# Converting 64-bit weights with two VectorE passes per piece instead of three

## The chip, the cores and the metric

The kernel runs on one core of a Trainium2 chip. The metric is the device time in microseconds; with one core it is that core's time from launch to end. A core has five engines with instruction queues of their own[...]: TensorE (PE; its weight loads are listed as PEld), VectorE (DVE), ScalarE (ACT), GpSimd (POOL) and SyncE (SP), which here only issues DMAs. They meet through semaphores.

## What is computed

A thresholded attention feeds a feed-forward block with an ELU in the middle. All tensors are 32-bit floats but the two weight matrices: they come from a product of an array with a 64-bit scalar and so arrive with 64 bits per element.

```python
scores = scale * np.matmul(q, k.transpose(0, 1, 3, 2))      # 8 x 8 heads, 576 x 576, head_dim 64
thresh = np.max(scores, axis=-1, keepdims=True) - tau
scores = np.where(scores >= thresh, scores, -1000000000.0)
scores = scores - np.max(scores, axis=-1, keepdims=True)
attn = np.exp(scores)
attn = attn / (np.sum(attn, axis=-1, keepdims=True) + 1e-09)
x = np.matmul(attn, v)                                      # as (4608, 512) tokens
h = x @ w_in                                                # w_in 512 x 2048, 64 bits
g = np.where(h > 0.0, h, np.exp(np.minimum(h, 0.0)) - 1.0)
out = g @ w_out                                             # w_out 2048 x 512, 64 bits
```

## The kernel before

Work on attention is cut into steps. A step is one block of 128 queries of a pair of heads (both heads), or the last 64 queries of both heads together; a pair takes five steps (the function calls carry `pr` for the pair and `i` for the block), four pairs make one sequence, and there are eight sequences. In a step, TensorE makes the scores of the two heads (L272), VectorE their maxima (L312), ScalarE the exponentials (L321, L323), VectorE the mask, which multiplies the exponentials by the comparison with the threshold and adds up the row sums (L332), then two short instructions for the reciprocals (L338, L339), and GpSimd the normalization (L308). In the next step TensorE transposes the weights of attention (L342), ScalarE copies them out of PSUM (L358), and for every second or third step TensorE multiplies them with the values (L477, L482), which ScalarE copies out (L599, L605).

[...]In the stages that concern us, the scores of the two heads take two banks each, and these come free when VectorE's mask has read them: so the scores of a step can't start before the masks of an earlier one.

The order of all engines is written out by hand, stage by stage, under `tc.manual_schedule()`; nothing is reordered afterwards. There are these stages:

- the first sequence (20 steps, to about 101 us). TensorE has idle-looking gaps that are filled with transposes of a constant tile, at places the code gives.
- the second stage, 15 steps (about 101 to 220 us), in which the feed-forward units of the first tokens are put between the attention work: `ffn1` (L640, with the exponential L647, GpSimd's minus one at L650 and VectorE's ELU at L654) and `ffn2_plain` (L680). `SHARES` says how many halves of a unit stand at which place in a step.
- later stages, in which the weights are in place as 32-bit numbers and the feed-forward products run in a form with fewer multiplications (L1133, L1273), with a planner that gives due times.

The conversion of the weights lies in the first two stages. They come in 32 pieces of 128 x 512 elements (16 of `w_in`, 16 of `w_out`), each with its two 32-bit words per element side by side: `staged[i]` is 128 x 512 x 2, so that the low words and the high words are each read with a stride of two words. `load_w` brings them in on SP's queue, into one of four buffers (`wst`). The work on piece `i` is cut into small functions, which the hand-written order calls at different places:

- `convert_rest` (L156): ScalarE turns the low word into the 3 bits and the rounding that it adds to a 32-bit number: low word times 2^-29, as an integer, in place.
- `convert_top`, which is `convert_shift` (L167) and `convert_sign` (L172): VectorE shifts the high word left by 3 and clears the top two bits, into `wtop` (two buffers); then it sets the top two bits from the high word.
- `convert_add` (L178): GpSimd adds the low word's share, as integers.
- `convert_abs` (L183): ScalarE takes the magnitude of the high word, read as a 32-bit float, in place.
- `convert_end` (L190): VectorE multiplies the sum by the comparison of that magnitude with a small bound, which makes numbers too small to matter exactly zero, and writes the result into `w_in_sb` or `w_out_sb`. It frees the buffer for the next load.

In the first stage the order places two pieces per pair of heads: for one, `convert_top`, `convert_add`, `convert_abs` stand in the pair's last step between the maxima and the mask, with `convert_end` in the next step; for the other, `convert_shift` stands at the end of one step, `convert_sign` and `convert_add` in the next, before its first mask. In this way 6 pieces are done. In the second stage each of the first 13 steps takes two pieces, `now[0]` and `now[1]`. The core of that step's order:

```python
if not behind_max: convert_top(now[0])          # else behind the maxima
finish_units(carried, slice(0, 2))              # exp, minus one of the step before
if not behind_max: convert_add(now[0])
early_ = ffn_halves(share[0])
...                                             # max_of, exp_of, bound_of for both heads; then the ELU
convert_abs(now[0])
after = ffn_halves(share[1])
convert_top(now[1]); convert_add(now[1]); convert_abs(now[1])
parts[1]()()                                    # transposes of the step before
second = ffn_halves(share[2])
carried = ffn_halves(share[3])
for h in hs: mask_of(pr, i, h)
reciprocal_of(pr, i, hs)
normalize(*step, hs)
for x in now: convert_end(x)
finish_units(after + second, slice(2, None))    # ELUs
```

`behind_max` holds in the first step of the stage and in the steps that also multiply with the values; there both pieces' `convert_top` stand behind the maxima, one straight after the other.

Of the kernel before, what the change touches and what calls it, by code (L numbers as in the profile page):

```python
# [10 lines left out]
FP32 = mybir.dt.float32  # L11
U32 = mybir.dt.uint32
I32 = mybir.dt.int32
AF = mybir.ActivationFunctionType
ALU = mybir.AluOpType
# [34 lines left out]
def kernel(  # L50
# [10 lines left out]
    nc = tc.nc  # L61
# [71 lines left out]
    pieces = [(moe_w_in, w_in_sb[:, j, n : n + WN], j, n) for n in range(0, DF, WN) for j in range(KJ)]  # L133
    pieces += [(moe_w_out, w_out_sb[:, f, n : n + WN], f, n) for f in range(NFT) for n in range(0, DM, WN)]
    staged, tops = {}, {}
# [16 lines left out]
    def convert_rest(i):  # L152

        if i in staged:
            lo = staged[i][:, :, 0]
            nc.scalar.mul(lo.bitcast(I32), lo, 2.0**-29)  # L156

    def convert_top(i):
        convert_shift(i)
        convert_sign(i)  # L160


    def convert_shift(i):
        if i in staged:
            hi = staged[i][:, :, 1]
            top = tops[i] = wstage.tile([P, WN], U32, name="wtop", bufs=2)
            nc.vector.tensor_scalar(top, hi, 3, 0x3FFFFFFF, ALU.logical_shift_left, ALU.bitwise_and)  # L167

    def convert_sign(i):
        if i in staged:  # L170
            hi, top = staged[i][:, :, 1], tops[i]
            nc.vector.scalar_tensor_tensor(top, hi, 0xC0000000, top, ALU.bitwise_and, ALU.bitwise_or)  # L172

    def convert_add(i):

# [3 lines left out]

    def convert_abs(i):  # L180
        if i in staged:
            mag = staged[i][:, :, 1].bitcast(FP32)
            nc.scalar.activation(mag, mag, AF.Abs)  # L183

    def convert_end(i):

        progress[1] = i + 1
        if i in staged:
            mag, top = staged.pop(i)[:, :, 1].bitcast(FP32), tops.pop(i).bitcast(FP32)
            nc.vector.scalar_tensor_tensor(pieces[i][1], mag, 1.125 * 2.0**-15, top, ALU.is_ge, ALU.mult)  # L190


    raws, pairs = {}, {}
# [553 lines left out]
    with tc.manual_schedule():  # L747
# [20 lines left out]
        for n in range(per_seq):  # L768
            pr, i = steps[n]
# [27 lines left out]
            if i == NB - 1 and n + 1 < per_seq:  # L797
                convert_top(x)
                convert_add(x)
                convert_abs(x)  # L800
                convert_rest(x + 1)
            elif i == 0 and n:
                convert_end(x)
                load_w()
            elif i == 1 and pr:
                convert_sign(x)
                convert_add(x)
            elif i in (2, 3):
                (prep_q if i == 2 else prep_k)(pr + 1)
                (copy_q if i == 2 else copy_k)(pr + 1)  # L810
# [17 lines left out]
            if i == 0 and n:  # L828
                convert_shift(x + 1)
            elif i == 2 and pr:  # L830
                convert_end(x)
                load_w()
            if i == 1 and pr:
                convert_abs(x)
            if i == 2 and n + 3 < per_seq:
                convert_rest(progress[1])
# [21 lines left out]
    with tc.manual_schedule():  # L858
# [3 lines left out]
        for n in range(per_seq, SWITCH):  # L862
            pr, i = step = steps[n]
            hs = heads_of(i)
            now = range(progress[1], min(progress[1] + 2, len(pieces)))
            if n == per_seq:
                for x in now:
                    convert_rest(x)
# [33 lines left out]
            for x in now[:1]:  # L902
                convert_abs(x)
# [20 lines left out]
            for x in now:  # L924
                convert_end(x)
# [103 lines left out]
    with tc.manual_schedule():  # L1029
        after = []  # L1030
        make_out(1), make_out(0)
        for n in range(SWITCH, MIDDLE):
            pr, i = steps[n]
# [507 lines left out]
```

## Time and profile before

| | us |
|---|---|
| median of 3 runs | 1335.6 (1333.85 to 1336.46) |
| the profiled execution | 1336.42 |
| its span, first to last instruction | 1334.3 |

The conversion's instructions in that execution, each 32 times:

| line | engine | what | median ns | lowest and highest |
|---|---|---|---|---|
| L156 | ScalarE | low word times 2^-29 | 690 | 662, 722 |
| L167 | VectorE | shift and AND | 421 | 382, 1232 |
| L172 | VectorE | sign bits in | 693 | 682, 1810 |
| L178 | GpSimd | integer add | 1294 | 1282, 1346 |
| L183 | ScalarE | magnitude | 684 | 647, 721 |
| L190 | VectorE | compare and multiply | 684 to 686 | 670, 1092 |

Busy time is the sum of an engine's instructions. TensorE's matmuls overlap, and a TensorE that is listed as busy may still be at half its clock, which the column PEclk shows (1.00 is the full clock). Idle time is put down to the instruction whose end released the waiting one. A wait of an engine costs time only if it lies on the way to the end of the kernel.

### The profile page before, as it was taken

What the parts mean: (1) busy time and instruction counts of PE and PEld (TensorE: products, weight loads), DVE (VectorE), ACT (ScalarE), POOL (GpSimd) and SP (SyncE); (2) the same over time, 40 slices, a digit from 0 to 9 for tenths busy, and PEclk for the clock granted to TensorE, in tenths of its full rate; (3) what the DMA queues carried; (4) which work ended last, traced back from release to release, by engine and by line L of the source; (5) the groups of instructions that cost most, each with busy time, mean ns of one, the idle gap of its engine ahead of it and who ended that gap; (6) DMA issues with size and microseconds to landing.
All of it is one profiled execution on the core that took longest, in us unless ns stands there. A gap on an engine that the chain in (4) does not pass through costs nothing.

```text
span 1334.3 us, 22146 instructions
## 1 busy us (share of the span) xinstructions
PE 1309.7 (98%) x6980; PEld 1014.8 (76%) x6980; DVE 1044.4 (78%) x2227; ACT 617.8 (46%) x1372; POOL 795.1 (60%) x1188
## 2 busy tenths in 40 slices
PE   9998999999999999999999999999999999999998
PEld 7665755746777778777777787778787887888887
DVE  6888895988888988888788878888889883545534
ACT  5777675225444444545453536363626361412320
POOL 4656774778657574756475737574766564624523
PEclk9998999999999999999999999999999999999999
DMA  6245452589787989898889898998888775221211
GB/s 119 60 98 143 132 162 48 178 249 257 191 247 210 248 239 240 211 260 237 232 224 261 232 241 231 245 249 227 230 235 251 216 218 190 106 72 56 95 59 32
DMA packets 322596, 247.77 MB, mean 186 GB/s; under 512 B 208688, under 2 KB 284464, under 8 KB 322480
## 3 DMA queue, kind: packets, MB, share of 16 engines
q1 hardware_dynamic: 320112, 246.07, 67.4%
q8 instruction: 55, 0.90, 0.3%
q10 hardware_dynamic: 2368, 0.30, 0.2%
q14 instruction: 61, 0.50, 0.1%
HBM read 161.81 MB, written 84.48 MB: 185 GB/s over the span
## 4 chain that ended last, share of the span: by engine, by line
PE 73%; DVE 1%; ACT 0%; issue 0%; POOL 0%; ACTq 0%
PE f L1273 29%; PE f L1133 27%; PE sc L529 8%; PE sc L589 7%; PE sc L581 1%; PE sc L576 1%; DVE wTa L1183 0%; DVE vm L1220 0%; DVE w L1220 0%; DVE wTb L1183 0%; POOL km L1173 0%; ACT w L546 0%; ACT xt L599 0%; ACT ge L1163 0%; POOL ge L1173 0%
## 5 line engine op out<-in xcount | busy, mean ns | idle before, releaser
L308 POOL TENSOR_SCALAR w<-w,rs 128x576 f32<-128x576 f32 x196 | 171.2, 880 | 102.2 <-DVE rs L339 84.7
L536 DVE TENSOR_REDUCE mx<-sc 128x1 f32<-128x576 f32 x207 | 149.2, 750 | 38.2 <-PE sc L529 30.3
L1133 PE MATMUL f<-xt,sw 128*128 128x256 f32 x512 | 125.6, 388 | 0.6 <-ACT xt L599 0.5
L1133 PE MATMUL f<-xt,w_in_sb 128*128 128x256 f32 x512 | 122.7, 382 | 0.8 <-ACT u L1147 0.8
L542 POOL TENSOR_SCALAR th<-mx,ntau 128x2 f32<-128x2 f32 (+1 forms) x115 | 34.0, 296 | 137.2 <-DVE mx L536 137.1
L529 PE MATMUL sc<-kT,qT 64*128 64x512 f32 (+4 forms) x736 | 109.5, 422 | 0.1
L541 ACT ACTIVATE nb<-mx,nkeep 128x2 f32<-128x2 f32 (+1 forms) x115 | 34.2, 298 | 161.4 <-DVE mx L536 161.4
L1133 PEld LDWEIGHTS f<-xt,w_in_sb 128*128 128x128 f32 x512 | 96.0, 190 | 16.8 <-ACT w L1147 2.8
L1133 PEld LDWEIGHTS f<-xt,sw 128*128 128x128 f32 x512 | 93.5, 190 | 20.0 <-DVE g L1155 5.0
L1273 PE MATMUL f<-w_out_sb,s 128*128 128x256 f32 x448 | 108.3, 383 | 0.0
L529 PEld LDWEIGHTS sc<-kT,qT 64*128 64x128 f32 x736 | 83.2, 186 | 32.1 <-issue 17.5
L1273 PE MATMUL f<-w_out_sb,g 128*128 128x256 f32 x448 | 107.1, 382 | 0.0
L1133 PE MATMUL f<-x,w_in_sb 128*128 128x256 f32 x448 | 106.3, 380 | 0.2 <-ACT s L1147 0.2
L550 DVE SCALAR_TENSOR_TENSOR w<-sc,th,w 128x576 f32<-128x576 f32 x115 | 90.0, 813 | 20.4 <-ACT w L546 17.4
L1273 PE MATMUL f<-t,s 128*128 128x256 f32 x448 | 105.8, 379 | 0.0
L416 DVE STREAM_TRANSPOSE x<-w 128x512 f32<-128x512 f32 (+2 forms) x143 | 96.5, 708 | 10.4 <-POOL w L308 7.4
L546 ACT ACTIVATE w<-sc,nb,keep 128x576 f32<-128x576 f32 x115 | 91.1, 831 | 14.1 <-DVE e L550 10.8
L1220 POOL TENSOR_TENSOR s<-g 128x256 f32<-128x256 f32 x104 | 80.4, 778 | 28.8 <-PE f L1273 20.1
L1273 PEld LDWEIGHTS f<-w_out_sb,g 128*128 128x128 f32 x448 | 84.1, 190 | 14.7 <-issue 3.8
L1273 PEld LDWEIGHTS f<-w_out_sb,s 128*128 128x128 f32 x448 | 83.8, 190 | 14.1 <-POOL s L1220 2.0
L1133 PEld LDWEIGHTS f<-x,w_in_sb 128*128 128x128 f32 x448 | 84.9, 190 | 12.7 <-issue 0.6
L1273 PEld LDWEIGHTS f<-t,s 128*128 128x128 f32 x448 | 85.1, 190 | 11.6
(196 smaller groups left out, 2976.8 us busy)
## 6 DMA issues: line engine op xcount, KB each, us to landing
there<-x SPq DMA_DIRECT2D x408, 144.0 KB, 3.7
wTb<-there SPq DMA_DIRECT2D x52, 576.0 KB, 6.4
wTa<-there SPq DMA_DIRECT2D x50, 576.0 KB, 4.7
sw<-win_sums SPq DMA_DIRECT2D x62, 384.0 KB, 4.2
t<-wout_sums SPq DMA_DIRECT2D x45, 512.0 KB, 5.7
qm<-in_q_dram SPq DMA_DIRECT2D x128, 72.0 KB, 4.5
vm<-in_v_dram SPq DMA_DIRECT2D x64, 128.0 KB, 2.9
wst<-in_moe_w_in_dram SPq DMA_DIRECT2D x16, 512.0 KB, 4.6
```

Source lines behind the costliest of these rows:

```text
L308: nc.gpsimd.tensor_scalar(wv, wv, st["rs"][:, h : h + 1], 1.0, ALU.mult, ALU.mult)
L416: nc.vector.transpose(x[:, :, c0 : c0 + nc_], src.rearrange("p (c g n) -> p g c n", c=nc_, n=T))
L529: on_banks(nc.tensor.matmul(o, qT[r, i * P : (i + 1) * P], kT[r, k0 : k0 + n], start=True, stop=True, skip_group_check=True), o)
L536: on_banks(nc.vector.tensor_reduce(st["mx"][:, h : h + 1], st["sc", h], axis=AX.XY if i == NC else AX.X, op=ALU.max), st["sc", h])
L541: nc.scalar.mul(st["nb"][:, cs], st["mx"][:, cs], nkeep)
L542: nc.gpsimd.tensor_scalar(st["th"][:, cs], st["mx"][:, cs], 1.0, ntau, ALU.mult, ALU.add)
L546: on_banks(nc.scalar.activation(st["e", h], st["sc", h], AF.Exp, bias=st["nb"][:, h : h + 1], scale=keep), st["sc", h])
L550: on_banks(nc.vector.scalar_tensor_tensor(st["e", h], st["sc", h], st["th"][:, h : h + 1], st["e", h], ALU.is_ge, ALU.mult, accum_out=st[" ...
L589: on_banks(nc.tensor.matmul(o, vm[:, h, c], parts[part][:, g0:g1, h * (NC + 1) + c], start=False, stop=(c == NC - 1), skip_group_check=Tru ...
L1133: nc.tensor.matmul(loc["banks"][place], left[:, j], right[:, j], start=(begins and j == 0), stop=(j == 1), skip_group_check=True)
L1220: engine.tensor_tensor(o, x, y, op)
L1273: nc.tensor.matmul(place(m), lhs, rhs, start=(begins and v == 0), stop=(v == RU - 1), skip_group_check=True)
```

## The change

VectorE's second pass per piece goes away. The high word is now shifted left by 3 without clearing bits, so that the sign and the top exponent bit fall off. ScalarE makes of the low word a 32-bit float between 2 and 4 (scale 2^-51, bias 2.0), whose bits, read as an integer, are 2^30 plus the low word's share; GpSimd's add, which is unchanged, so gives the bits of the magnitude. The sign, and zero for very small numbers, come from the high word, read as a float, through a steep tanh that is written as an integer and so rounds to -1, 0 or 1. VectorE's last pass multiplies the magnitude (at least 0.0) by it.

`convert_sign` stays as an empty function; where `convert_top` or `convert_sign` are called is as before.

```diff
     def convert_rest(i):
         if i in staged:
             lo = staged[i][:, :, 0]
-            nc.scalar.mul(lo.bitcast(I32), lo, 2.0**-29)
+            nc.scalar.activation(lo.bitcast(FP32), lo, AF.Copy, scale=2.0**-51, bias=2.0)
...
     def convert_shift(i):
         if i in staged:
             hi = staged[i][:, :, 1]
             top = tops[i] = wstage.tile([P, WN], U32, name="wtop", bufs=2)
-            nc.vector.tensor_scalar(top, hi, 3, 0x3FFFFFFF, ALU.logical_shift_left, ALU.bitwise_and)
+            nc.vector.tensor_scalar(top, hi, 3, None, ALU.logical_shift_left)
 
     def convert_sign(i):
-        if i in staged:
-            hi, top = staged[i][:, :, 1], tops[i]
-            nc.vector.scalar_tensor_tensor(top, hi, 0xC0000000, top, ALU.bitwise_and, ALU.bitwise_or)
+        pass
...
     def convert_abs(i):
         if i in staged:
-            mag = staged[i][:, :, 1].bitcast(FP32)
-            nc.scalar.activation(mag, mag, AF.Abs)
+            hi = staged[i][:, :, 1]
+            nc.scalar.activation(hi.bitcast(I32), hi.bitcast(FP32), AF.Tanh, scale=0.5493 / (1.06 * 2.0**-15))
...
     def convert_end(i):
         progress[1] = i + 1
         if i in staged:
-            mag, top = staged.pop(i)[:, :, 1].bitcast(FP32), tops.pop(i).bitcast(FP32)
-            nc.vector.scalar_tensor_tensor(pieces[i][1], mag, 1.125 * 2.0**-15, top, ALU.is_ge, ALU.mult)
+            sign, top = staged.pop(i)[:, :, 1].bitcast(I32), tops.pop(i).bitcast(FP32)
+            nc.vector.scalar_tensor_tensor(pieces[i][1], top, 0.0, sign, ALU.max, ALU.mult)
```

## The prediction

> **What bounds the kernel now.** I read the page first, then busy time by stretch, then the waits and the timeline of those stretches that hold the conversion (its lines L156 to L190 run from 22.8 to 212.3 us and nowhere else).
>
> ```profile
> PE 1309.7 (98%) x6980; PEld 1014.8 (76%) x6980; DVE 1044.4 (78%) x2227; ACT 617.8 (46%) x1372; POOL 795.1 (60%) x1188
> ```
>
> The page says TensorE: 98% busy, 73% of the chain that ended last, and behind 219 us nothing else. The change touches VectorE, so it can only pay where TensorE waits. Stretches of the second stage:
>
> ```profile
> core 0: us, PE busy (x) PEld busy (x) DVE busy (x) ACT busy (x) POOL busy (x), PEclk, DMA share, GB/s
> 101.00:118.26 17.26, 12.86 (x55) 6.37 (x53) 13.78 (x27) 10.54 (x25) 10.28 (x13) 0.80 0.41 126
> 118.26:141.88 23.62, 23.36 (x131) 18.02 (x130) 22.34 (x40) 17.81 (x37) 16.29 (x21) 1.00 0.65 172
> 141.88:154.67 12.79, 11.16 (x48) 8.74 (x47) 11.13 (x23) 8.59 (x21) 9.52 (x10) 0.87 0.29 87
> 154.67:219.50 64.83, 62.59 (x290) 35.25 (x290) 58.55 (x111) 44.76 (x93) 46.91 (x54) 1.00 0.40 112
> ```
>
> VectorE is busy 105.8 of 118.5 us, which looks like the bound; but TensorE is full in the second row and nearly in the fourth. What a faster VectorE can return there is TensorE's idle time, not VectorE's. Its waits from 101 to 219.5 us, and the granted clock around the two long ones (same columns):
>
> ```profile
> PE sc L272 <- DVE w L332: 6.1, 4, 4.1
> PE f L640 <- DVE g L654: 1.6, 1, 1.6
> ```
>
> ```profile
> 104.30:108.40 4.10, 0.00 (x0) 0.01 (x1) 4.03 (x8) 3.87 (x10) 2.42 (x3) 1.00 0.16 65
> 108.60:115.30 6.70, 6.70 (x20) 2.98 (x21) 6.41 (x13) 3.45 (x7) 4.50 (x6) 0.51 0.48 157
> 146.10:149.40 3.30, 3.30 (x12) 2.72 (x11) 3.23 (x7) 0.53 (x2) 1.61 (x2) 0.53 0.52 190
> ```
>
> After each long wait the clock is half for 6.8 and 3.4 us: a wait is paid twice. The first, in the timeline (start, length, engine, line, idle before):
>
> ```profile
> 104.37 0.42 DVE L167 TENSOR_SCALAR wtop<-wst 128x512 uint32<-128x512 uint32 x1
> 104.82 0.69 DVE L172 SCALAR_TENSOR_TENSOR wtop<-wst,wtop 128x512 uint32<-128x512 uint32 x1
> 105.43 0.42 DVE L167 TENSOR_SCALAR wtop<-wst 128x512 uint32<-128x512 uint32 x1
> 105.65 1.33 POOL L178 TENSOR_TENSOR wtop<-wtop,wst 128x512 int32<-128x512 int32 x1 [0.73 <-DVE wtop L172]
> 105.89 1.65 DVE L172 SCALAR_TENSOR_TENSOR wtop<-wst,wtop 128x512 uint32<-128x512 uint32 x1
> 107.46 0.81 DVE L332 SCALAR_TENSOR_TENSOR w<-sc,th,e 128x576 f32<-128x576 f32 x1
> 108.42 3.00 PE L272 MATMUL sc<-kT,qT 64*128 64x288 f32 x8 [4.15 <-DVE w L332]
> ```
>
> Two sign passes (L172), the second stretched from 0.69 to 1.65 us by POOL's add, stand before the mask (L332) that frees the banks for the next scores. The second wait is the ELU (L654) behind two stretched end passes:
>
> ```profile
> 142.61 1.96 DVE L190 SCALAR_TENSOR_TENSOR w_in_sb<-wst,wtop 128x512 f32<-128x512 f32 x2
> 144.50 0.68 DVE L654 SCALAR_TENSOR_TENSOR g<-g,f 128x512 f32<-128x512 f32 x1
> 145.22 2.76 PE L640 MATMUL f<-xt,w_in_sb 128*128 128x256 f32 x8 [1.63 <-DVE g L654]
> ```
>
> [...]1.65 us for the sign pass that met POOL's add, 0.69 alone. [...]Here Abs takes 684 ns and the scaled copy 690 (medians of L183, L156); no tanh is shown. [...]The half-clock stretches here are 6.8 and 3.4 us long, and the second followed a wait of only 1.6 us.
>
> **The change, part by part.** Durations are of the profiled execution, 1336.42 us (span 1334.3, 2.1 around it); the median of the runs is 1335.6, so 0.8 comes off at the end.
>
> Same-for-same edits, cost 0. The scaled copy gets an immediate bias: the same form with a bias, L1175, takes 624 ns against 690, so from 0.07 less to 0; I take 0. Tanh for Abs: 0, by the two rows above; its upper end is rival D. The shift without its AND (median 421 ns): from 0 to +0.27, if it fell to the 0.69 of a two-input pass; 0[...]. The end pass with an integer operand (0.69): from 0 to +0.12, the next longer two-input row (the 576-element mask, 0.81); 0. Both upper ends together are 0.39 x 26 = 10.1 us of VectorE time, less than half of what goes; only (b) below would feel them, by 0.5. The order of the built program shows each engine's instructions unchanged but for 32 fewer on VectorE, and one table load in both. No DMA moves.
>
> Removed: 32 sign passes, 28.9 us of VectorE: 6 (4.1 us) before 101 us, 26 (24.8 us) after. POOL's add and ScalarE's in-place pass now wait for the shift alone. By place:
>
> (a) First stage, 6 passes. They lie beside the exponential: sign 60.40 to 61.08, exponential until 61.01, mask at 61.11. Nothing there. But the sign held POOL's small nb (L786, 0.64 instead of 0.26), so the normalization behind it, for which TensorE waits (2.1 us in three waits, the one at 61.98 for 0.74), comes 0.3 earlier: 3 x 0.3 = 0.9 at best, 0 at worst; I take 0.7.
>
> (b) First step of the second stage. Without signs: shift to 104.79, shift to 105.24, then the exponential is late next, ready at 105.79 (it starts at 104.96 and takes 0.83): mask at 105.83 instead of 107.46, scores at 106.87 instead of 108.42: 1.55.[...]
>
> (c) The step behind it. TensorE's idle time is still 2.6 us, so I expect the clock still to halve. But the scores (until 108.55) now run ahead of it; values 5.25 us as now, 108.65 to 113.9; turns 1.9; next scores at 115.8 instead of 118.26: 2.4 with (b). If the clock holds, VectorE sets it: end passes to 109.4, maxima to 110.9, two shifts to 112.6, mask to 113.4, scores at 113.5: 4.7 with (b).
>
> (d) 118.26 to 141.88: TensorE idle 0.26 us. I take 0.1; what VectorE saves here becomes its idle time.
>
> (e) 141.88 to 154.67. The single-head step before ends on VectorE 0.5 earlier (its mask at 140.9 to 141.05 instead of 141.49, behind a shift that took 1.23); the add no longer queues behind a sign, so POOL's minus starts at 141.65 instead of 142.97; the ELU ends at 143.7 instead of 145.18. 1.5 off the wait. The rest, some 0.6 of idle time, is too little to halve the clock (1.22 at 193.1 us did not): 3.4 us at half are 1.7 saved. Sum 3.2; 1.5 if it halves anyway.
>
> (f) 154.67 to 219.5: 64.83 less 62.59 is 2.2 idle, 1.22 of it at 193.07, where a sign (192.96 to 193.65) stands before the mask. The others (0.30 at 178.2, 0.41 at 210.4, 0.30 at 211.4) end on the same chain, and at 171.8 the scores' loads wait 0.44 for a mask. I take 2.0, of 1.0 to 3.0.
>
> Sum: 0.7 + 2.4 + 0.1 + 3.2 + 2.0 = 8.4. Behind 219.5 TensorE runs full (12.80 of 12.80 us to 232.3) and all later waits are relative, so the shift stays whole. 28.9 us of work taken away gives 8.4: TensorE is late next.
>
> **Rivals.**
> B, the clock never halves: 2.3 more, 1324.9. For it: the idle time shrinks from 4.15 to 2.6. Against: 1.6 sufficed at 146.
> C, TensorE's waits end on something else: exponentials (ScalarE held four of the later masks 0.2 to 0.6 us), POOL's adds, which start earlier[...]. Then only (b) and about 1 us more: 2.5 off, 1333.1. For it: ScalarE and POOL are busy 81.7 and 83.0 of 118.5 us, and POOL's count is unchanged. Against: both lose waits for the sign.
> D, slower: tanh swaps ScalarE's table against exp. Price: the one ACT_TABLE_LOAD here, 1.283 us. Between tanhs of the second stage stand exponentials: 13 to 26 groups, two loads each, 33 to 67 us on ScalarE against its 36.8 idle; it decides from some 29 loads on. With 67 the stage is 30 longer: 1366. Against it: one load in the built program.
>
> **Numbers.** Chances: the sum 0.56, B 0.17, C 0.20, D 0.07. Time 1335.6 - 8.4 = 1327.2. Range 1323.5 (B with all of (a) and (f)) to 1333.0 (most of the way into C). About 0.2%, 2.7 us, is what measurement tells from no change: faster 0.56 + 0.17 + half of C = 0.83, same 0.10, slower 0.07.
>
> **What would show it.** TensorE's wait near 107 us should fall from 4.15 to some 2.6, the one at 145 to under 1, the one at 193 go; the half clock at 146 go, the one at 108.5 perhaps stay; no VectorE row of 1.6 us; VectorE's busy time down by some 25 to 29 us and its idle time in the second stage up by 15 or more; the first stage within 1 us of now; one table load; from 219.5 on the same length. Wrong, if the second stage ends on time although the sign passes are gone (C), or if ScalarE shows rows over 0.75 us for the new passes.

## The result, and the profile after

| | before | after |
|---|---|---|
| median of 4 runs each, same chip | 1335.23 us (1333.85 to 1336.46) | 1328.6 us (1327.35 to 1329.12) |
| ratio of the two, 95% interval | | 0.9949 [0.9932, 0.9966] |
| the profiled execution | 1336.42 | 1328.54 |
| its span | 1334.3 | 1326.6 |

The changed kernel is 6.6 us faster by the medians (4.5 to 9.1 by the interval) and 7.7 us by the spans of the two profiled executions. The forecast was 8.4. Line numbers of the changed kernel are one or two lower than before in the parts shown here: the scores are L271, the masks L331, the exponentials L322, the copies out of PSUM L357, the ELU L653, the add L176, the tanh L181, the end pass L189.

The page's busy times, all engines:

```profile
PE 1306.3 (98%) x6980; PEld 1012.8 (76%) x6980; DVE 1018.8 (77%) x2195; ACT 616.3 (46%) x1372; POOL 789.5 (60%) x1188
```

VectorE has 32 instructions and 25.6 us less; nothing else has changed its count. What each new form costs is in the groups by line (line, engine, operation, out<-in, count | busy us, mean ns | idle before):

```profile
L167 DVE TENSOR_SCALAR wtop<-wst 128x512 uint32<-128x512 uint32 x32 | 15.5, 500 | 0.0
L181 ACT ACTIVATE wst<-wst 128x512 int32<-128x512 f32 x32 | 20.8, 678 | 0.0
L156 ACT ACTIVATE wst<-wst 128x512 f32<-128x512 uint32 x32 | 20.7, 692 | 0.0
L320 ACT ACT_TABLE_LOAD x1 | 1.3, 1283 | 2.9 <-issue 2.9
```

The tanh that writes integers takes 678 ns where the magnitude took 684, the copy with its bias 692 against 690, and there is one table load, as before. The end pass with an integer operand has a median of 684 ns, as before. The median of the shift is 420 ns (421 before); its mean of 500 comes from ten of 0.45 to 1.23 us, in each of which GpSimd was at work on its add (five) or its normalization (five).

TensorE's time by stretch. The four rows are the same work as the four rows that the prediction showed of before (the first two steps of the second stage, the next three, the sixth, and the rest of that stage):

```profile
core 0: us, PE busy (x) PEld busy (x) DVE busy (x) ACT busy (x) POOL busy (x), PEclk, DMA share, GB/s
99.84:115.54 15.70, 12.85 (x55) 6.45 (x54) 10.07 (x23) 10.40 (x25) 11.21 (x13) 0.78 0.44 138
115.54:138.86 23.32, 23.13 (x130) 18.09 (x129) 19.86 (x39) 18.77 (x39) 17.40 (x22) 1.00 0.69 176
138.86:147.94 9.08, 9.01 (x47) 7.22 (x47) 7.28 (x16) 7.11 (x17) 6.40 (x8) 1.00 0.33 116
147.94:211.85 63.91, 61.77 (x290) 34.79 (x290) 47.36 (x98) 44.76 (x94) 45.07 (x54) 1.00 0.40 114
211.80:1326.60 1114.80, 1105.71 (x5807) 877.34 (x5805) 860.07 (x1847) 466.76 (x1056) 656.03 (x976) 1.00 0.73 201
```

The last row is 1114.80 us long, exactly as long as from 219.5 us to the end before, with TensorE busy 1105.71 against 1105.67: whatever the first two stages gained was kept to the end. In the stage above it VectorE's busy time fell from 105.8 to 84.6 us, while ScalarE's (81.7 to 81.0) and GpSimd's (83.0 to 80.1) hardly moved. The granted clock in the third row went from 0.87 to 1.00; in the first row it did not recover (0.80 to 0.78).

The same by steps of attention, each from its first matmul of the scores to that of the next step (worked out from the trace; steps are counted from 0, so step 20 is the first of the second stage):

| steps | before, us | after, us | gained |
|---|---|---|---|
| 6, 11, 16 (a piece with the sign pass before the mask) | 4.78 + 4.78 + 5.03 | 4.41 + 4.41 + 4.41 | 1.36 |
| 20 | 7.13 | 5.57 | 1.56 |
| 21 | 9.84 | 9.84 | 0 |
| 22 to 24 | 23.62 | 23.33 | 0.29 |
| 25 | 12.79 | 9.08 | 3.71 |
| 26 to 33 | 64.91 | 63.98 | 0.93 |
| start of step 0 | 7.93 | 8.16 | -0.23 |

The sum is 7.62 of the 7.7. All other steps of the first stage agree within 0.02 us.

TensorE's waits in the second stage of the changed kernel (waiter, what it waited for: us in total, times, longest):

```profile
PE sc L271 <- DVE w L331: 4.5, 5, 2.6
```

The wait for the ELU (1.6 before) is gone from the list; that for the mask fell from 6.1 to 4.5, its longest from 4.1 to 2.6. That longest one, in the timeline of step 20 (start, length, engine, line, idle before):

```profile
103.20 0.76 DVE L167 TENSOR_SCALAR wtop<-wst 128x512 uint32<-128x512 uint32 x2
103.97 2.54 POOL L176 TENSOR_TENSOR wtop<-wtop,wst 128x512 int32<-128x512 int32 x2
104.72 0.82 DVE L331 SCALAR_TENSOR_TENSOR w<-sc,th,e 128x576 f32<-128x576 f32 x1 [0.76 <-ACT e L322]
105.69 1.28 PE L271 MATMUL sc<-kT,qT 64*128 64x288 f32 x2 [2.59 <-DVE w L331]
```

The two shifts now run back to back, the adds come only behind them and so hold up nothing on this path, and VectorE then sits idle for 0.76 us until the exponential is done. Behind the wait the clock is still halved (same columns as the stretches above):

```profile
105.60:112.20 6.60, 6.50 (x18) 2.99 (x20) 6.14 (x15) 4.96 (x12) 5.72 (x7) 0.51 0.48 155
```

### The profile page after: what moved, and what is told of

It reads as the page before. It is cut to its first block, busy times and chain, and to the rows that moved or that the text cites. A ratio compares the mean times of both kernels' runs of the same rounds, so it can differ in the third digit from the quotient of the medians.

```text
span 1326.6 us, 22126 instructions
## 1 busy us (share of the span) xinstructions
PE 1306.3 (98%) x6980; PEld 1012.8 (76%) x6980; DVE 1018.8 (77%) x2195; ACT 616.3 (46%) x1372; POOL 789.5 (60%) x1188
## 4 chain that ended last, share of the span: by engine, by line
PE 90%; DVE 3%; DMA 2%; ACT 2%; SPq 1%; issue 1%; POOL 1%; DVEq 0%; ACTq 0%; POOLq 0%
PE f L1272 29%; PE f L1132 28%; PE sc L528 8%; PE sc L588 7%; PE rt L341 4%; PE sc L271 4%; PE f L639 3%; PE f L679 2%; PE pv L481 2%; DMA there<-x 1%; PE sc L580 1%; PE sc L575 1%; PE pv L476 1%; SPq L444 1%; ACT e L322 1%
## 5 line engine op out<-in xcount | busy, mean ns | idle before, releaser
L1272 PE MATMUL f<-t,s 128*128 128x256 f32 x448 | 105.8, 379 | 0.0
L1132 PEld LDWEIGHTS f<-x,w_in_sb 128*128 128x128 f32 x448 | 84.9, 190 | 12.7 <-issue 0.5
```

What stands on the lines that cost most here:

```text
L1132: nc.tensor.matmul(loc["banks"][place], left[:, j], right[:, j], start=(begins and j == 0), stop=(j == 1), skip_group_check=True)
L1272: nc.tensor.matmul(place(m), lhs, rhs, start=(begins and v == 0), stop=(v == RU - 1), skip_group_check=True)
```

## The experiments

Three questions were open. Is the gain made by the few sign passes that stand ahead of a wait of TensorE, or by VectorE's lighter load as a whole? How much of it is idle time and how much the clock? And why did the steps from 26 on, where 2.0 us were expected, give 0.9? My theory was the places; the first rival was that the gain goes with the busy time removed.

### Seven pieces in the new form, and the other 25

Pieces 1, 3, 5 (steps 6, 11, 16), 6 and 7 (step 20), 14 and 15 (step 24) are those whose sign passes the prediction had put ahead of TensorE's waits up to step 25. One kernel converts only these seven in the new form, its counterpart only the other 25; each function takes the old or the new form by piece. The diff is that of the seven, against the changed kernel.

```diff
+    NEW = (1, 3, 5, 6, 7, 14, 15)
...
     def convert_sign(i):
-        pass
+        if i in staged and i not in NEW:
+            hi, top = staged[i][:, :, 1], tops[i]
+            nc.vector.scalar_tensor_tensor(top, hi, 0xC0000000, top, ALU.bitwise_and, ALU.bitwise_or)
```

(`convert_rest`, `convert_shift`, `convert_abs` and `convert_end` branch in the same way.)

> Only seven of the 32 pieces are converted the new way (1, 3, 5, 6, 7, 14, 15), the other 25 keep the sign pass. If the gain is TensorE's waits (theory), it stays nearly whole: the steps of pieces 1, 3 and 5 go from 4.78, 4.78, 5.03 us to about 4.4 each, the first step of the second stage from 7.1 to 5.6, and the step behind pieces 14 and 15 from 12.8 to about 9.1 with no half clock there; together about 6.4 us off the span. If the gain follows VectorE's busy time (rival), 7 of 32 passes bring about 7/32 of 7.7, that is 1.7 us.

Measured: 1330.95 us against 1336.46, ratio 0.9957 [0.994, 0.9973], 5.5 us less. VectorE lost only some 4 of its 184.2 us of the first 220. Steps 6, 11 and 16 took 4.41 us each and step 20 5.58: what the whole change gave there. In step 25, which took 9.67 us, the wait for the ELU fell from 1.63 to 0.66 us and no half clock followed (in this kernel the ELU is L667, its user L653):

```profile
PE f L653 <- DVE g L667: 0.7, 1, 0.7
```

Step 21 took 8.71, since this time the half clock lasted 3.41 instead of 6.83 us, behind the same wait of 2.6 us. By step 26 it had gained 7.0 us (1.1 of it by the shorter half clock), as much as the whole change had by then. It lost some of this later: in step 31 a wait of 1.23 us, which before is 1.22 and left the clock alone, was followed by a half clock of 3.41 us:

```profile
189.90:193.10 3.20, 3.20 (x10) 1.17 (x12) 3.13 (x7) 2.57 (x5) 3.20 (x5) 0.52 0.74 274
```

> The complement: 25 of the 32 pieces the new way, the seven of the other run (1, 3, 5, 6, 7, 14, 15) with the sign pass. Theory: VectorE loses some 22 us of work and the span only about 1.2 us (0.3 before the step at 142 us, 0.9 behind 155 us); both half-clock stretches stay. Rival, by VectorE's busy time: 25/32 of 7.7, that is 6.0 us off. The first stage should be as in the kernel before, which shows that pieces 0, 2 and 4 bring nothing.

Measured: 1332.75 us, ratio 0.997 [0.9958, 0.9982], 3.7 less, where my theory had 1.2. The first stage and step 20 were as before (4.78, 4.78, 5.04 and 7.13 us), as expected, and the half clock behind step 20 stayed. What I had wrong was step 25: 9.87 us, although pieces 14 and 15 still had their sign passes (line numbers as in the run with the seven):

```profile
PE f L653 <- DVE g L667: 0.9, 1, 0.9
```

The wait was 0.86 us instead of 1.63, and no half clock followed:

```profile
141.29:151.16 9.87, 9.01 (x48) 7.22 (x46) 8.08 (x16) 6.98 (x18) 7.25 (x10) 1.00 0.32 107
```

So two things made the wait: the seven take 0.97 of the 1.63 us away, through the signs of pieces 14 and 15, and the other 25 take 0.77, through the pieces of the steps before, whose work VectorE still had in its queue: it ended step 23's end passes 2.3 us behind the start of step 24 in the kernel before and with the seven, and 0.8 us behind it here. Together that is the whole wait, and either alone was enough to save the half clock, whose 1.7 us (shown below) thus count in both halves. Mainly for this the two halves of the change, 4.8 and 4.1 us by their spans, add up to more than the whole. Most of the rest that the 25 gained is 0.81 us in step 28.

The rival falls with both: by busy time the seven should have given 7/32 of 7.7, or 1.7 us, and the others 6.0.

### The half clock taken away: in the changed kernel behind step 20, in the kernel before in step 25

`idle(14)` is the kernel's own filler, 14 transposes of the constant tile. Behind step 20 of the changed kernel it fills most of TensorE's wait for the masks; in the kernel before it stands ahead of the feed-forward products of step 25, where they wait for the ELU. In the changed kernel:

```diff
+            if n == per_seq:
+                idle(14)
         finish_units(carried, ALL)
```

and in the kernel before:

```diff
+            if n == per_seq + NB:
+                idle(14)
             early_ = ffn_halves(share[0])
```

> The changed kernel with 14 transposes of the constant tile behind the first step of the second stage, on TensorE, where it waits 2.6 us for the mask. If the half clock behind that wait is what keeps the next step at 9.84 us (theory), the clock stays full, that step falls to 7.0 to 7.7 us, and the time is 2 to 2.8 us under the changed kernel's, about 1326. If VectorE or the loads set that step (rival), it stays at 9.8 although the clock is full, and the time does not move, or rises by some tenths.

Measured: 1326.18 us, ratio 0.9923 [0.9908, 0.9938]: 2.4 less than the first result of the changed kernel, which was not measured beside it, and 3.2 less than its second (below). Steps 20 and 21 (the stretches are laid 0.24 us ahead of the steps):

```profile
101.28:106.77 5.49, 4.97 (x32) 3.33 (x30) 2.74 (x5) 3.58 (x9) 2.80 (x5) 1.00 0.58 187
106.77:113.86 7.09, 6.30 (x35) 3.18 (x35) 6.57 (x17) 6.51 (x17) 6.39 (x7) 1.00 0.46 147
```

Step 20 kept its length, step 21 fell from 9.84 to 7.09 at the full clock. So the half clock behind step 20 costs the changed kernel 2.75 us by the profiles, and 2.4 to 3.2 by the medians.

> The kernel before with 14 transposes of the constant tile on TensorE in the wait near 143 us, behind that step's scores; the conversion is untouched. The transposes fill the wait and cannot shorten it. If the half clock behind it cost 1.7 of the 3.7 us that the change gained there (theory), the step falls from 12.79 to about 11.1 us and the time by about 1.7. If the whole gain there was the shorter wait (rival), the step stays at 12.8 or grows.

Measured: 1334.64 us, ratio 0.9986 [0.9979, 0.9993], 1.8 less. Step 25:

```profile
142.20:153.30 11.10, 11.10 (x62) 9.01 (x60) 10.26 (x22) 8.14 (x20) 8.97 (x10) 1.00 0.37 100
```

It has the clock at 1.00 and takes 11.1 us instead of 12.8, although the ELU comes no sooner (it ends 3.3 us behind the start of the step in both): the transposes only fill the wait. So of the 3.7 us that the change gained in step 25, 1.7 are the clock, and the other 2.0 the 1.6 of wait and small gaps.

### The changed kernel once more, and with the copies behind the exponentials

In the changed kernel, ScalarE's exponential is what TensorE's wait now hangs on, in step 20 and in step 30. Step 30 (the view and columns of the timeline above):

```profile
183.14 0.60 PE L341 MATMUL rt<-ident,w 128*128 128x128 f32 x4
183.77 0.65 ACT L357 COPY wTb<-rt 128x256 f32<-128x256 f32 x2 [2.11 <-PE rt L341]
...
184.64 0.83 ACT L322 ACTIVATE e<-sc,nb,keep 128x576 f32<-128x576 f32 x1
185.59 0.82 DVE L331 SCALAR_TENSOR_TENSOR w<-sc,th,e 128x576 f32<-128x576 f32 x1 [2.38 <-ACT e L322]
186.56 0.72 PE L271 MATMUL sc<-kT,qT 64*128 64x288 f32 x2 [0.89 <-DVE w L331]
```

VectorE waits 2.38 us for the exponential. ScalarE could have made it earlier, but it stood for 2.11 us at the copies out of PSUM, which wait for TensorE's transposes and come before the exponential in its order. The experiment puts these copies behind the exponentials in the first step of every pair in this stage (steps 20, 25 and 30), and is compared with the changed kernel run again beside it.

```diff
-            if not valued:
+            if not valued and i:
                 copies()
...
             if valued:
                 out_values()
                 copies()
+            elif not i:
+                copies()
```

> The changed kernel once more, as the yardstick of this call: about 0.995 of the kernel before, with a half-clock stretch of 3.4 or 6.8 us behind the first step of the second stage and none at the step that lasted 12.8 us before.

Measured: 1329.35 us, ratio 0.9951 [0.9936, 0.9966], the first result again. Its trace has step 25 at 9.08 us, and the half clock behind step 20 for 6.83 us, this time beginning 0.9 us behind the start of the scores instead of together with it. Step 21 was not shorter for that but 10.26 us.

> The changed kernel with ScalarE's copies of the first transposes put behind the exponentials in those steps of the second stage that follow a single-head step. Theory: the wait that stayed near 186 us (0.89 and 0.33 us) is ScalarE's: the exponential queues behind copies that wait for TensorE's transposes; moved, the maxima alone decide, the mask comes some 1.5 us earlier and both waits go, about 1.0 to 1.2 us off. Rival: VectorE or GpSimd's adds hold it, or the later copies hold the next transposes: no change within 0.3 us, or slower by the same.

Measured: 1326.44 us, ratio 0.9931 [0.9914, 0.9947], 2.9 less than the run beside it, where 1.0 to 1.2 were expected. Step 30:

```profile
182.10 0.83 ACT L322 ACTIVATE e<-sc,nb,keep 128x576 f32<-128x576 f32 x1
183.05 0.82 DVE L331 SCALAR_TENSOR_TENSOR w<-sc,th,e 128x576 f32<-128x576 f32 x1 [0.25 <-ACT e L322]
183.88 0.64 ACT L357 COPY wTb<-rt 128x256 f32<-128x256 f32 x2
```

The mask comes right behind the exponential, and TensorE's waits of that step are gone: steps 30 and 31 take 5.46 and 8.89 us instead of 6.42 and 9.89, 2.0 less. Step 20 takes 4.77 instead of 5.58: its wait is down to 1.79 us. The clock was still halved behind it for 6.83 us, and step 21 took 10.01. I had expected about one of these 2.0 us; that the mask's lateness is handed on to step 31 I had not seen.

### Both, and both with the filler in a bank of its own

> The changed kernel with both the 14 transposes behind the first step of the second stage and the moved copies: if the two are independent, 2.4 and 1.0 us add up, about 3.4 us under the changed kernel's time, some 0.9925 to 0.992 of the kernel before, with no half clock from 10 us to the last microseconds. If the moved copies only shift the wait, it equals the run with the transposes alone.

The two edits together: 1325.1 us, ratio 0.9922 [0.9907, 0.9937], 4.25 less than the changed kernel beside it. That is more than the 3.4 us expected, but less than the sum of what each edit had given alone. The clock stayed full from the first step to 1320.1 us, but steps 20 and 21 took 7.01 and 6.05 us, 13.06 together, where the filler alone had 12.58. TensorE in step 20:

```profile
105.76 1.42 PE L341 MATMUL rt<-ident 128*128 128x128 f32 x11 [2.35 <-ACT wTb L357]
```

The filler writes into a PSUM bank (the unit in which this kernel hands out PSUM) of the transposes, which comes free when the copies have read it. With the copies moved behind the exponentials, the filler itself waits for them, 2.35 us, and then stands in front of the scores. The last kernel gives it a free bank of the feed-forward products:

```diff
-            if n == per_seq:
-                idle(14)
+            if n == per_seq:
+                rt = bank()
+                for _ in range(13):
+                    transpose(rt[:, :P], ident)
```

> As the run with both edits, but 13 transposes of the constant tile, into a bank of the feed-forward units, which is free there. If in that run the transposes started late because their bank waited for the moved copies (7.01 and 6.05 us for the two steps, against 4.77 for the first of them with the copies alone), then here they start at once, the two steps together fall from 13.1 to 11 to 12 us with no half clock, and the time goes 1 to 2 us under that run's, about 0.991 of the kernel before. If the copies themselves hold the scores, the two steps stay at about 13.

Measured: 1324.2 us (1324.04 to 1326.47, five runs), ratio 0.991 [0.9896, 0.9924]; the lowest median here, though the interval overlaps with that of the run with both edits, which was not measured beside it. Its TensorE in step 20:

```profile
103.08 1.58 PE L341 MATMUL f<-ident 128*128 128x128 f32 x13
105.03 0.72 PE L271 MATMUL sc<-kT,qT 64*128 64x288 f32 x2 [0.37 <-DVE w L331]
```

The filler starts at once, as expected. Steps 20 and 21 take 4.77 and 7.47 us, 12.24 together, a little over the 11 to 12 expected, and the clock is not halved before 1321.2 us, at the kernel's end.

## Why the prediction was right, point by point

**The bound.** TensorE, as said: of 28.9 us taken off VectorE by the forecast (25.6 off the page's busy time) 7.7 came back. The other 17.9 became idle time of VectorE: in the second stage this rose from 12.7 to 27.4 us, just under the 15 more that had been named. The seven pieces show that it is the place that counts.

**Same-for-same edits at 0.** Right for all four; none is longer by more than 0.02 us in the median. That tanh and the shift by itself would take no longer was my estimate, from the 684 and 690 ns of two other functions and the 421 ns of the shift with its AND; they took 679 and 420. There is an exception: a shift that meets GpSimd's add is stretched. This happens off the path of the scores in steps such as 24, where one shift took 1.23 us:

```profile
134.28 1.28 POOL L176 TENSOR_TENSOR wtop<-wtop,wst 128x512 int32<-128x512 int32 x1
134.63 1.23 DVE L167 TENSOR_SCALAR wtop<-wst 128x512 uint32<-128x512 uint32 x1
```

The shift ends 0.29 us behind the end of the add, and takes 0.42 us alone. Three more shifts that began while an add ran took 0.56 to 0.57 us and ended 0.28 to 0.29 us behind it; one that began ahead of its add (151.48 us, the add at 151.71) took 0.42. In the kernel before, six sign passes of 0.69 us alone took 1.65 to 1.81 where an add ran, and ended 0.55 us behind it. What holds them back was not shown.

**(a) First stage, 0.7 of at most 0.9.** It gave 1.36 in the three steps. The mechanism was right (TensorE's waits for the normalization fell from 2.1 to 1.1 us, and GpSimd's small instruction took 0.27 us instead of 0.64 in each of the three), the size was not: I took at most 0.3 for each, and two steps gave 0.37 and one 0.62. The first stage so became 1.2 us shorter, more than the "within 1 us" among the signs. A later start by 0.23 us, ahead of any changed instruction, took part of it back in this pair of profiles.

**(b) First step of the second stage, 1.55.** It gave 1.56, and by the chain forecast: shift, shift, exponential, mask, scores. (The forecast's own times have the mask 1.63 and the scores 1.55 earlier; counted from the start of the step, the trace has 1.57 and 1.56.) GpSimd's adds came only behind both shifts (from 103.97 us, the shifts from 103.20), which took 0.76 us together; neither was stretched.

**(c) The step behind it, 0.85.** It gave 0. This term failed, by its reasoning too. I had left the half clock where it was in time and let the scores run ahead of it. But it came earlier together with the wait: it began at 105.71 us instead of 108.76, and lasted 6.83 us in both profiles. Nor did it help where more of the scores ran ahead of it: in the second trace of the changed kernel it began 0.9 us behind their start instead of together with it, and step 21 took 10.26 us instead of 9.84. What could have been saved here was its whole price by rival B, 2.75 us with the filler; with the wait of 2.6 us that stayed, B did not come true.

**(d) 0.1.** It gave 0.29, nearly all in step 24.

**(e) 3.2.** It gave 3.71: no half clock, 1.7 as priced, shown by the filler in the kernel before, and 2.0 for waits and gaps where I had 1.5. The ELU ended 1.3 us behind the start of the step instead of 3.3, so 2.0 earlier where I had 1.5, and nothing was left of the 0.6 us of idle time that I left standing (my own figures, a wait of 1.63 less 1.5, leave only 0.1). The reason was too narrow. I named the passes and the add of the step just before; the runs with seven and with 25 pieces show that the earlier steps' passes delayed the ELU nearly as much. And "too little to halve the clock", drawn from the wait of 1.22 us, was no safe ground: in the run with the seven one of 1.23 us was followed by a half clock of 3.41 us.

**(f) 2.0 of 1.0 to 3.0.** It gave 0.93, just under the range of the term, and 0.81 of this lies in step 28, where the loads of the scores had waited for the second mask:

```profile
171.84 0.78 PEld L272 LDWEIGHTS sc<-kT,qT 64*128 64x128 f32 x6 [0.44 <-DVE w L332]
```

This wait went, and the scores of step 28 fell from 1.97 to 1.24 us. Steps 30 and 31, where I had 1.2, gave 0.12 together. Here rival C came true, in one place: the wait of 1.22 us at 193 us, which I let go whole, came back as 0.89 and a smaller one of 0.33, since the exponential is late next, held by the copies of PSUM ahead of it. With the copies moved, both go, and 2.0 us with them; 0.8 us of the wait in step 20 went in the same way.

**Rival D.** One table load, no row of the tanh over 0.72 us. Nothing of it was seen. (One of the 32 scaled copies took 0.757 us, just over the 0.75 named as a sign of being wrong; their median is 690 ns.)

So the total was off by 0.7 between the profiled executions, from (c) by 0.85 and (f) by 1.1 too much, (a), (d) and (e) by 1.4 too little, and the later start. That it came so close is in part luck: 1.9 us too much in two terms stood against 1.4 too little in three. The medians differ by 1.1 us less than the profiles do. Part of such differences is the clock too: the second profile of the changed kernel has a further half clock of 3.41 us at 8.8 us, in its very first step, which took 5.00 instead of 3.44 us, while the next took 4.48 instead of 5.21; 0.8 us were lost. Whether this makes up the whole of the 1.1 was not tested.

## What to carry to other kernels

When work is taken off an engine that is not the bound, add up the waits of the bounding engine that this work ended, not its busy time: seven of the 32 passes gave 5.5 of the 6.6 us here. For each such wait ask what is second latest, and look in that engine's order for something that waits without need, such as a copy ahead of an exponential; moving it paid 2.9 us with no work removed. A wait of TensorE is to be priced with the half clock that may follow it (2.75 us behind the wait of 2.6 us here), and filling it with idle transposes, in a bank that nobody holds, can pay even where the wait itself can't be shortened (1.8 us in the kernel before).

## What had not been expected of the hardware

The clock was halved behind waits of TensorE of 4.15 and 1.63 us in the kernel before, of 2.6 in the changed kernel and the run with the seven, of 1.79 in the run with the copies moved, and once, in the run with the seven, behind one of 1.23 us; not behind 1.22 in the kernel before, nor behind 0.66 and 0.86 in the runs with the seven and with the 25, nor behind one of 2.35 us in the run with both edits. The half clock lasted 3.41 or 6.83 us, and the wait of 2.6 us led to 6.83 in one kernel and 3.41 in the other, with the same code around it. So the length of a wait alone did not tell what it cost.

The records of the clock in the profiles of before and after show how these half clocks lie. They begin at 108.76, 146.30 and, at the kernel's end, 1334.14 us in the kernel before, 11.00 and then 348.00 times 3.413 us apart; and at 105.71 and 1324.27 us in the changed kernel, 357.00 times 3.413 us apart. TensorE's matmuls in the 3.41 us right ahead of each:

| kernel | stretch, us | matmuls busy, us | half clock behind it, us |
|---|---|---|---|
| before | 105.34 to 108.76 | 0.34 | 6.83 |
| before | 142.89 to 146.30 | 1.78 | 3.41 |
| before | 1330.73 to 1334.14 | 0.00 | to the kernel's end |
| after | 102.30 to 105.71 | 0.82 | 6.83 |
| after | 1320.86 to 1324.27 | 0.51 | to the kernel's end |

Cut the two profiles into stretches of this length on the same beat, from the first record of the clock at 6.4 and 6.7 us on. Of all the other stretches at full clock, one of the kernel before had 1.74 us of matmuls (from 1327.32 us), and every other had 2.2 us or more; the clock was halved behind none of them. That a stretch with 1.78 us was followed by half the clock and one with 1.74 was not leaves open what else decides it.

The wait of 1.63 us lay whole in the stretch with 1.78 us of matmuls. The one of 1.22 us in the kernel before was cut by the beat at 194.09 us into 0.78 and 0.44; the two stretches had 2.63 and 2.96 us of matmuls.

Where the filler stood in the wait, the clock stayed full: at 1.00 in steps 20 and 21 of the changed kernel with it (TensorE busy for 4.97 of 5.49 and 6.30 of 7.09 us), in step 25 of the kernel before (11.10 of 11.10), and from 9 to 1318 us in the last kernel.

What makes a half clock 3.41 or 6.83 us long was not found. What a wait of 1.2 to 2.6 us cost beyond itself was here anything from nothing to the 3.2 us by which step 21 grew with 6.83 us at half the clock (10.26 us in the second trace of the changed kernel, 7.09 with the filler).
